# An mLSTM and gated feed-forward kernel: the opening's order of work is rewritten

## The chip, the cores and the metric

The kernel runs on one core of one Trainium2 chip. The metric is the device time of one execution in microseconds, the median of several runs; smaller is better. The engines are named as in the profile: PE (TensorE, matmuls and transposes), PEld (its weight loads), DVE (VectorE), ACT (ScalarE), POOL (GpSimd) and SP (SyncE, which issues the DMAs).

## The reference

Two steps, both in fp32. The first is an mLSTM over 4 batches, 8 heads, 768 time steps and a head size of 40:

```python
for t in range(S):
    kt, vt, qt = (k[:, :, t], v[:, :, t], q[:, :, t])
    m_new = np.maximum(f_gate[:, :, t] + m, i_gate[:, :, t])
    f_stab = np.exp(f_gate[:, :, t] + m - m_new)
    i_stab = np.exp(i_gate[:, :, t] - m_new)
    m = m_new
    C = f_stab[:, :, None, None] * C + i_stab[:, :, None, None] * np.einsum('bhd,bhe->bhde', vt, kt)
    n = f_stab[:, :, None] * n + i_stab[:, :, None] * kt
    h_tilde = np.einsum('bhde,bhe->bhd', C, qt)
    nq = np.einsum('bhd,bhd->bh', n, qt)[:, :, None]
    denom = np.maximum(np.abs(nq), 1.0)
    o = 1.0 / (1.0 + np.exp(-o_gate[:, :, t]))
    y[:, :, t] = o * h_tilde / denom
```

Its output, 3072 tokens of 320 numbers (batch by time), goes through a gated feed-forward:

```python
gate = 1.0 / (1.0 + np.exp(-(x @ w_gate)))
val = x @ w_val
return (gate * val @ w_out).astype(np.float32)
```

with an inner width of 1536.

## The kernel before, in words

The 768 time steps are cut into 6 chunks of 128. A chunk of one batch is a *unit*: unit n is chunk n // 4 of batch n % 4, so units 0 to 3 are the first chunk of batches 0 to 3. Inside a chunk the recurrence is done as attention: scores of q and k (128 x 128 per head), multiplied with a decay matrix `d`, then with v; a state of 40 x 41 per head is carried from chunk to chunk. The feed-forward works on the output of a chunk, 128 or 256 or 512 tokens wide, in 12 blocks of 128 of the inner width. In the first chunk the first four blocks are done for batches 0 and 1 alone, as soon as these are there.

All matmuls of the feed-forward are exact enough for fp32 by a split in two: each operand x is written as `xh` (rounded) and `xl` (the rest), and three products are summed. The same holds for the weights, which arrive as raw 64-bit words and are unpacked in the kernel.

The order of all work is written out by hand: the table `ORDER` (L47 on) is a string of names, and the kernel emits the operation of each name in that order. Each engine then runs its own operations in that order, one behind the other, and waits by semaphores for what others produce. The table `eng` in `PARAM` says for some names which engine does it ('v' DVE, 'p' POOL, 'a' ACT). The number behind a name is the unit, the weight piece or the feed-forward block. The names that matter here:

- `ee3.0`, `ee3.1` (L657, ACT): exponents of the decay matrix of batch 3, four heads each, in place in the tile `d_3`, which a DMA fills (`d<-mscr`). `em3` (L671, POOL) then sets the upper triangle to zero; `kw3` (L881, POOL) multiplies unit 3's k with a column of it.
- `tr` (L762, PE) and `cp` (L770 on ACT, L772 on DVE): the transposes of q and k of a unit, and the copies of them out of PSUM.
- `s` (L690, PE): scores; `t` (L872, DVE): scores times decay; `av` (L938, PE): times v; `cs` (L1014, PE) and `cm` (L1043, ACT): the state.
- `nd`, `ns`, `ro` (L951 to L962, DVE): the output gate and the denominator; `ro` writes the tile `x`. `xd` (L987): a copy of 64 columns inside `x`; `xt` (L993, PE): transposes of `x` into PSUM; `xh` (L1000, ACT) and `xl` (L1004, DVE): the two parts, input of the feed-forward.
- `u0`, `u1` (L1070, PE): three products of two matmuls each with the gate weights (`u0`) or the value weights (`u1`); `r0`, `r1` (L1074, L1075): the last 64 rows of them. `th` (L1080, ACT), `gx` (L1087, DVE), `gh` (L1092, ACT), `gl` (L1097, DVE): the gate, the product and its two parts; `dn` (L1107 to L1109, PE): the second matmul, three products, of which the third needs `gl`.
- weights: `wa` (L517, ACT), `wb` (L521, DVE), `wc` (L526, DVE), `wo` (L531, DVE) unpack a piece into the staging tile `dc`; `wh` (L543, ACT) writes the rounded part and `wl` (L548, POOL) the rest. The piece is named behind: g gate weights, v value weights, r the last rows, o the output weights (whose two parts are shown as `oh` and `ol`); `wlo1` is the rest of output piece 1.
- `gm5`, `gd` (L427, L428, L438, DVE): the running maximum of the gates over the chunks; `tb` (L448 on PE, L453 on DVE): its transposes.
- `wk` (L404, PE): bf16 matmuls on zeros, spread over the opening, which write a PSUM tile that nobody reads. `wm` (L394, PE): eight fp32 matmuls on zeros, likewise.

Buffers are handed out in turn by the helpers `sbt` and `pst`: a name with k buffers gets them one after the other in the order of the table, and whoever takes a buffer waits for the readers of its last content. The staging tiles `dc` have 3 buffers; the PSUM tiles of `tr`, `s` and `tb` (tag `pa`) have 2; `x` has one. The tile `sg` of block 0, which `th0` writes, has the place in SBUF where the padded k of unit 3 lies before, which `kw3` reads.

Of the kernel before, what the change touches and what calls it, by code (L numbers as in the profile page):

```python
# [37 lines left out]
    'NW': 12,  # L38
    'eng': {
# [3 lines left out]
    },  # L43
}
# [4 lines left out]
    wav0 lk0 gc tap tac sp0.1 ee0.0 lk1 gm1 sp1.0 wco0 lq1 wcr0 ee0.1 kw0 lo0 tr0.1 wor0 whr0 wbv0 wlr0 gm2 lv0 i5  # L49
    tr0.0 sp1.1 cp0.0 cp0.1 s0.0 tr1.0 woo0 wdo4 gm3 lo1 ee1.0 ee1.1 cp1.0 wdo1 ld2 l10 tr1.1 kw1 wcv0 wov0 t0.0 lv1  # L50
    lq3 wdg0 cp1.1 wao4 tr2.0 l11 cp2.0 s1.0 who0 gm4 cs0 wlo0 wbo4 wco4 t0.1 whv0 av0 t1.0 og1 wlv0 og0 cm0.1 t1.1
    lk2 wao1 ld3 wbo1 woo4 ee2.1 who4 wco1 wlo4 woo1 wk4 av1 ee2.0 wdg1 em2 nd0 ns0 gs1 wk5 cm0.0 ro0 wk6 wdo3 wag0
    nd1 ns1 tr3.0 cp3.0 xd0 wbg0 lk3 lv2 l12 tr2.1 xt0 cp2.1 ro1 wcg0 kw2 ee3.1 wk7 xh0 wk8 who1 wk9 gm5 xd1 i8 wk10
    lo2 xt1 wdr1 wog0 xh1 xl0 wk11 xl1 wag1 ld4 wdv1 wbg1 wm gd s2.0 t2.0 t2.1 whg0 u1.0 r1.0 wlo1 tbp tbc wlg0
    tr3.1 lq4 wao3 wbo3 cp3.1 ee3.0 u0.0 r0.0 war1 og2 em3 lv3 kw3 lo3 th0 wco3 wcg1 woo3 wdo5 cs1 wbr1 cm1.1 who3
    wlo3 lk4 wog1 gx0 cm1.0 whg1 gh0 lq5 av2 ns2 ee4.0 u0.1 ee4.1 gl0 r0.1 th1 dn0.0 nd2 l13 wcr1 ro2 s3.0 wor1 t3.0
    t3.1 wlg1 u1.1 r1.1 wav1 wbv1 cs2 wcv1 wdv3 wao5 wbo5 u0.2 wov1 xd2 cm2.1 tr4.0 wco5 cm2.0 em4 cp4.0 gx1 whv1
# [1104 lines left out]
```

## Time and profile before

| what | value |
|---|---|
| median of 3 runs | 518.9 us (518.62 to 519.23) |
| span of the profiled execution | 517.4 us (the 1.5 us to the median lie around the span) |
| PE busy | 506.7 us (98%) |
| PEld busy | 468.3 us (91%) |
| DVE busy | 332.8 us (64%) |
| ACT busy | 242.1 us (47%) |
| POOL busy | 246.3 us (48%) |
| chain that ended last | PE 89%, DMA 5%, ACT 2%, DVE 2% |

The profile lists, for one execution, what each engine did and when; the span is the time from its first to its last instruction. Starts are counted from the beginning of the span. An operation that stands as x4 is four instructions in a row, and the duration is that of all of them together. In brackets behind a row stands the idle time of the engine before it and what ended it. Starts of neighbouring rows can lie closer than the first one's duration, because an engine takes up the next instruction while the last one is still finishing.

### The profile page before, as it was taken

The numbers are of one execution on the slowest core, as the hardware profiler recorded it, in microseconds if no ns is written. First come the engines' busy times: TensorE is split into PE (matmuls) and PEld (weight loads), VectorE is DVE, ScalarE is ACT, GpSimd is POOL, SyncE is SP. The second block draws the span as 40 slices with busy tenths as digits, with TensorE's granted clock in tenths as the row PEclk, the third lists the DMA queues.
The fourth block names the chain that finished last, engine by engine and source line by source line (L and its number), as shares of the span: only waits on it lengthen the run. The fifth ranks groups of instructions, "written<-read, shape, count | busy, mean of one in ns | idle before, by whom it ended". The sixth has DMA issues, their size and how long they took to land.

```text
span 517.4 us, 11006 instructions
## 1 busy us (share of the span) xinstructions
PE 506.7 (98%) x4020; PEld 468.3 (91%) x4021; DVE 332.8 (64%) x699; ACT 242.1 (47%) x560; POOL 246.3 (48%) x272
## 2 busy tenths in 40 slices
PE   6989999999999999999999999999999999999997
PEld 4789988889999999998888888898888888999996
DVE  7978877785776677678766456856445474642332
ACT  4887766554444354644444443353344324232322
POOL 3656546557146686459536544187315504510000
PEclk9999999999999999999999999999999999999999
DMA  8999875339687797799879787599465835220000
GB/s 196 259 231 225 223 201 141 102 95 178 135 185 156 166 203 163 162 205 158 171 138 178 181 153 141 135 181 185 96 146 102 173 81 111 65 58 1 1 27 27
DMA packets 222478, 74.17 MB, mean 143 GB/s; under 512 B 167380, under 2 KB 214168, under 8 KB 222424
## 3 DMA queue, kind: packets, MB, share of 16 engines
q1 hardware_dynamic: 221336, 73.20, 64.8%
q8 instruction: 32, 0.52, 0.4%
q10 hardware_dynamic: 1088, 0.26, 0.2%
q14 instruction: 22, 0.18, 0.1%
HBM read 61.54 MB, written 11.90 MB: 142 GB/s over the span
## 4 chain that ended last, share of the span: by engine, by line
PE 89%; DMA 5%; ACT 2%; DVE 2%; issue 1%; SPq 1%; POOL 0%; POOLq 0%; DVEq 0%; ACTq 0%
PE pg L1070 38%; PE po L1107 8%; PE po L1109 8%; PE po L1108 7%; PE pg L1074 6%; PE pg L1075 6%; PE av L931 3%; PE s L753 2%; PE av L938 2%; DMA d<-mscr 2%; PE in L914 2%; PE cs L1014 2%; PE s L808 1%; DMA st_v<-in_moe_w_val_dram 1%; DMA scx<-tx 1%
## 5 line engine op out<-in xcount | busy, mean ns | idle before, releaser
L1092 ACT ACTIVATE gh<-pg 128x256 fp32r<-128x256 f32 (+1 forms) x103 | 48.2, 468 | 142.9 <-DVE pg L1087 120.7
L1087 DVE SCALAR_TENSOR_TENSOR pg<-sg,pg 128x256 f32<-128x256 f32 (+1 forms) x103 | 54.8, 532 | 92.1 <-PE pg L1075 75.4
L1070 PE MATMUL pg<-xh,wh 128*128 128x256 f32 (+1 forms) x412 | 104.8, 336 | 0.2 <-ACT xh L1000 0.2
L1070 PE MATMUL pg<-xh,wl 128*128 128x256 f32 (+1 forms) x412 | 100.9, 326 | 0.0
L1070 PE MATMUL pg<-xl,wh 128*128 128x256 f32 (+1 forms) x412 | 100.8, 326 | 0.0
L1107 PE MATMUL po<-oh,gh 128*128 128x320 f32 x288 | 92.6, 322 | 0.0
L1109 PE MATMUL po<-oh,gl 128*128 128x320 f32 x288 | 89.1, 309 | 0.1
L1108 PE MATMUL po<-ol,gh 128*128 128x320 f32 x288 | 88.9, 309 | 0.0
L1080 ACT ACTIVATE sg<-pg 128x256 f32<-128x256 f32 (+1 forms) x103 | 48.1, 467 | 73.3 <-PE pg L1075 71.9
L1097 DVE TENSOR_TENSOR gl<-pg,gh 128x256 fp32r<-128x256 f32 (+1 forms) x103 | 54.3, 527 | 36.6 <-ACT gh L1092 34.9
L1070 PEld LDWEIGHTS pg<-xl,wh 128*128 128x128 f32 x412 | 69.1, 189 | 7.3 <-POOL xl L1004 0.3
L1070 PEld LDWEIGHTS pg<-xh,wl 128*128 128x128 f32 x412 | 69.0, 189 | 7.1
L1070 PEld LDWEIGHTS pg<-xh,wh 128*128 128x128 f32 x412 | 67.7, 189 | 3.7 <-DVE gl L1097 0.6
L1074 PE MATMUL pg<-xh,w 128*128 128x256 f32 (+1 forms) x206 | 68.5, 333 | 0.0
L1075 PE MATMUL pg<-xl,w 128*128 128x256 f32 (+1 forms) x206 | 67.0, 326 | 0.0
L1107 PEld LDWEIGHTS po<-oh,gh 128*128 128x128 f32 x288 | 54.4, 189 | 2.5
L1108 PEld LDWEIGHTS po<-ol,gh 128*128 128x128 f32 x288 | 54.2, 188 | 2.6
L1109 PEld LDWEIGHTS po<-oh,gl 128*128 128x128 f32 x288 | 54.1, 188 | 0.7 <-DVE gl L1097 0.6
L671 POOL TENSOR_SCALAR_AFFINE_SELECT d<-d 128x1024 f32<-128x1024 f32 x22 | 26.2, 1192 | 52.6 <-ACT d L667 51.9
L887 POOL TENSOR_TENSOR dr<-d 128x1024 f32<-128x1024 f32 x16 | 30.3, 1894 | 35.7 <-DVE d L872 35.3
L872 DVE TENSOR_TENSOR d<-s,d 128x384 f32<-128x384 f32 (+2 forms) x68 | 34.9, 527 | 14.5 <-PE s L753 8.9
L1075 PEld LDWEIGHTS pg<-xl,w 128*128 128x128 f32 x206 | 39.0, 189 | 2.7
(159 smaller groups left out, 886.2 us busy)
## 6 DMA issues: line engine op xcount, KB each, us to landing
d<-mscr SPq DMA_DIRECT2D x22, 512.0 KB
ks<-scq SPq DMA_DIRECT2D x48, 168.0 KB
qs<-scq SPq DMA_DIRECT2D x48, 168.0 KB
scq<-tq SPq DMA_DIRECT2D x64, 80.0 KB
su_o<-in_moe_w_out_dram SPq DMA_DIRECT2D x12, 320.0 KB
o<-in_o_gate_dram SPq DMA_DIRECT2D x24, 160.0 KB
v<-in_v_dram SPq DMA_DIRECT2D x24, 160.0 KB
out_dram<-ob SPq DMA_DIRECT2D x24, 160.0 KB
```

Source lines behind the costliest of these rows:

```text
L872: nc.vector.tensor_tensor(y, ps_[n, g][:, :nh, :], y, ALU.mult)
L887: E("da", n).tensor_tensor(dr[n][0], dm[n], top(dm[n]), ALU.subtract)
L1070: nc.tensor.matmul(p, w[y][:, a, fs], x[c][:, a, n0:n1], start=(i + a == 0), stop=False)
L1074: nc.tensor.matmul(pg[n, y], w2[y][:, fs], xh[c][:, 2, n0:n1], start=False, stop=False)
L1075: nc.tensor.matmul(pg[n, y], w2[y][:, fs], xl[c][:, 2, n0:n1], start=False, stop=True)
L1080: nc.scalar.activation(s, pg[n, 0], AF.Tanh, scale=0.5)
L1087: nc.vector.scalar_tensor_tensor(sgs[n], gate, 1.0, pg[n, 1], ALU.add, ALU.mult)
L1092: nc.scalar.activation(ghs[n][:, :nt], sgs[n], AF.Copy)
L1097: E("gl", n).tensor_tensor(gls[n][:, :nt], sgs[n], ghs[n][:, :nt].bitcast(F32), ALU.subtract)
L1107: nc.tensor.matmul(p, ghs[n][:, ts], oh[:, j, :], start=(j == 0), stop=False)
L1108: nc.tensor.matmul(p, ghs[n][:, ts], ol[:, j, :], start=False, stop=False)
L1109: nc.tensor.matmul(p, gls[n][:, ts], oh[:, j, :], start=False, stop=(j == NF - 1))
```

## The change

Four lines of the order table are rewritten, one name gets another engine, and one name is left out:

```diff
--- before.py
+++ after.py
@@ -38,7 +38,7 @@
     'NW': 12,
     'eng': {
         'gl': 'v', 'ca': 'v', 'ro': 'v', 'cm': 'a', 'cp0': 'a', 'cp2': 'a', 'qb2': 'v', 'dl0': 'v', 'cp11': 'a',
-        'qb00': 'v', 'qb10': 'v', 'qb20': 'v', 'qb01': 'v', 'qb21': 'p', 'xd0': 'v', 'ea0': 'a', 'ea1': 'a', 'ea2': 'a',
+        'qb00': 'v', 'qb10': 'v', 'qb20': 'v', 'qb01': 'v', 'qb21': 'p', 'xd0': 'v', 'xd1': 'v', 'ea0': 'a', 'ea1': 'a', 'ea2': 'a',
         'ea3': 'a', 'pz': 'v', 'gc': 'v', 'gd': 'v', 'ea4': 'a', 'ea5': 'a', 'ea6': 'a', 'ea7': 'a',
     },
 }
@@ -49,9 +49,9 @@
     wav0 lk0 gc tap tac sp0.1 ee0.0 lk1 gm1 sp1.0 wco0 lq1 wcr0 ee0.1 kw0 lo0 tr0.1 wor0 whr0 wbv0 wlr0 gm2 lv0 i5
     tr0.0 sp1.1 cp0.0 cp0.1 s0.0 tr1.0 woo0 wdo4 gm3 lo1 ee1.0 ee1.1 cp1.0 wdo1 ld2 l10 tr1.1 kw1 wcv0 wov0 t0.0 lv1
     lq3 wdg0 cp1.1 wao4 tr2.0 l11 cp2.0 s1.0 who0 gm4 cs0 wlo0 wbo4 wco4 t0.1 whv0 av0 t1.0 og1 wlv0 og0 cm0.1 t1.1
-    lk2 wao1 ld3 wbo1 woo4 ee2.1 who4 wco1 wlo4 woo1 wk4 av1 ee2.0 wdg1 em2 nd0 ns0 gs1 wk5 cm0.0 ro0 wk6 wdo3 wag0
-    nd1 ns1 tr3.0 cp3.0 xd0 wbg0 lk3 lv2 l12 tr2.1 xt0 cp2.1 ro1 wcg0 kw2 ee3.1 wk7 xh0 wk8 who1 wk9 gm5 xd1 i8 wk10
-    lo2 xt1 wdr1 wog0 xh1 xl0 wk11 xl1 wag1 ld4 wdv1 wbg1 wm gd s2.0 t2.0 t2.1 whg0 u1.0 r1.0 wlo1 tbp tbc wlg0
+    lk2 wao1 ld3 wbo1 woo4 ee2.1 who4 wco1 wlo4 woo1 wk4 av1 ee2.0 wdg1 em2 nd0 ns0 gs1 wk5 cm0.0 ro0 xd0
+    wk6 wdo3 xt0 wag0 nd1 ns1 ro1 lk3 lv2 l12 xd1 xt1 xh0 wbg0 xl0 tr3.0 xh1 cp3.0 xl1 tr2.1 cp2.1 wcg0 kw2 wk7 wk8
+    wk9 gm5 i8 wk10 lo2 wdr1 wog0 wk11 who1 ld4 wdv1 whg0 wlg0 u1.0 r1.0 wag1 wbg1 ee3.1 gd s2.0 t2.0 t2.1 wlo1 tbp tbc
     tr3.1 lq4 wao3 wbo3 cp3.1 ee3.0 u0.0 r0.0 war1 og2 em3 lv3 kw3 lo3 th0 wco3 wcg1 woo3 wdo5 cs1 wbr1 cm1.1 who3
     wlo3 lk4 wog1 gx0 cm1.0 whg1 gh0 lq5 av2 ns2 ee4.0 u0.1 ee4.1 gl0 r0.1 th1 dn0.0 nd2 l13 wcr1 ro2 s3.0 wor1 t3.0
     t3.1 wlg1 u1.1 r1.1 wav1 wbv1 cs2 wcv1 wdv3 wao5 wbo5 u0.2 wov1 xd2 cm2.1 tr4.0 wco5 cm2.0 em4 cp4.0 gx1 whv1
```

`xd1`, the 64-column copy of unit 1, goes from POOL to DVE. The names `xd0 xt0 nd1 ns1 ro1 xd1 xt1 xh0 xl0 xh1 xl1` come ahead of `tr3.0`, `cp3.0`, `tr2.1`, `cp2.1` and `ee3.1`. `u1.0 r1.0` come ahead of `s2.0`. `whg0 wlg0` come ahead of `u1.0`, `wag1`, `ee3.1` and `wlo1`. `wm` is dropped.

On ACT, from `wag0` (`dc_g<-st_g`) to `war1` (`dc_r`), before:

```order
L517 ACTIVATE dc_g_387<-st_g_288 128x512
L770 ACTIVATE qkt_399<-pt_0_394 128x512
L657 ACTIVATE d_342<-d_342,at 128x128 x4
L1000 ACTIVATE xh_427<-xt_412 128x3x128
L543 ACTIVATE oh<-dc_o_340 128x320
L1000 ACTIVATE xh_427<-xt_441 128x3x128
L517 ACTIVATE dc_g_453<-st_g_369 128x512
L543 ACTIVATE wh_100<-dc_g_387 128x2x256
L517 ACTIVATE dc_o_508<-su_o_385 128x320
L657 ACTIVATE d_342<-d_342,at 128x128 x4
L517 ACTIVATE dc_r_525<-su_r_445 128x256
```

and now:

```order
L517 ACTIVATE dc_g_392<-st_g_288 128x512
L1000 ACTIVATE xh_410<-xt_388 128x3x128
L1000 ACTIVATE xh_410<-xt_406 128x3x128
L770 ACTIVATE qkt_421<-pt_0_415 128x512
L543 ACTIVATE oh<-dc_o_340 128x320
L543 ACTIVATE wh_100<-dc_g_392 128x2x256
L517 ACTIVATE dc_g_464<-st_g_369 128x512
L657 ACTIVATE d_342<-d_342,at 128x128 x4
L517 ACTIVATE dc_o_499<-su_o_386 128x320
L657 ACTIVATE d_342<-d_342,at 128x128 x4
L517 ACTIVATE dc_r_516<-su_r_443 128x256
```

`qkt` is `cp3.0`, the two L657 rows are `ee3.1` and `ee3.0`, the L1000 rows `xh0` and `xh1`, `oh` is `who1`, `wh_100` is `whg0`, and `dc_o` behind the exponents is `wao3`. Both `xh` now stand ahead of `ee3.1`, which stands behind `whg0` and `wag1`; `wao3` still follows it. In these rows and the next the number behind a tile tells which of several it is; it differs between the two kernels.

On POOL, from `kw2` (k of unit 2) to `wlg1`, before:

```order
L881 TENSOR_TENSOR k_420<-pad_97,d_272 128x320
L987 COPY x_417<-x_417 128x64
L548 TENSOR_TENSOR ol<-dc_o_340,oh 128x320
L548 TENSOR_TENSOR wl_101<-dc_g_387,wh_100 128x2x256
L671 AFFINE_SELECT d_342<-d_342 128x1024
L881 TENSOR_TENSOR k_531<-pad_99,d_342 128x320
L548 TENSOR_TENSOR ol<-dc_o_508,oh 128x320
L609 MEMSET v_529 128x8
L548 TENSOR_TENSOR wl_101<-dc_g_453,wh_100 128x2x256
```

and now:

```order
L881 TENSOR_TENSOR k_431<-pad_97,d_272 128x320
L548 TENSOR_TENSOR wl_101<-dc_g_392,wh_100 128x2x256
L548 TENSOR_TENSOR ol<-dc_o_340,oh 128x320
L671 AFFINE_SELECT d_342<-d_342 128x1024
L881 TENSOR_TENSOR k_522<-pad_99,d_342 128x320
L548 TENSOR_TENSOR ol<-dc_o_499,oh 128x320
L609 MEMSET v_520 128x8
L548 TENSOR_TENSOR wl_101<-dc_g_464,wh_100 128x2x256
```

The copy `xd1` is gone from POOL, and `wlg0` (`wl_101`) stands ahead of `wlo1` (`ol`), where it stood behind it.

On DVE, the twelve rows that end with `t2.0` and `t2.1` (L872), before:

```order
L772 COPY qkt_299<-pt_1_407 128x512
L962 TENSOR_TENSOR x_417<-o_257,den_389 128x320
L526 TENSOR_SCALAR dc_g_387<-dc_g_387 128x512
L427 SCALAR_TENSOR_TENSOR mg<-gin,mend 32x128
L428 TENSOR_TENSOR mend<-gin,mg 32x1
L531 SCALAR_TENSOR_TENSOR dc_g_387<-st_g_288,dc_g_387 128x512
L1004 TENSOR_TENSOR xl_428<-xt_412,xh_427 128x3x128
L1004 TENSOR_TENSOR xl_428<-xt_441,xh_427 128x3x128
L521 TENSOR_SCALAR dc_g_453<-dc_g_453 128x512
L438 TENSOR_TENSOR gin<-mend,mg 32x640
L872 TENSOR_TENSOR d_272<-s_0_470,d_272 128x4x128
L872 TENSOR_TENSOR d_272<-s_1_471,d_272 128x4x128
```

and now:

```order
L521 TENSOR_SCALAR dc_g_392<-dc_g_392 128x512
L1004 TENSOR_TENSOR xl_411<-xt_388,xh_410 128x3x128
L1004 TENSOR_TENSOR xl_411<-xt_406,xh_410 128x3x128
L772 COPY qkt_299<-pt_1_424 128x512
L526 TENSOR_SCALAR dc_g_392<-dc_g_392 128x512
L427 SCALAR_TENSOR_TENSOR mg<-gin,mend 32x128
L428 TENSOR_TENSOR mend<-gin,mg 32x1
L531 SCALAR_TENSOR_TENSOR dc_g_392<-st_g_288,dc_g_392 128x512
L521 TENSOR_SCALAR dc_g_464<-dc_g_464 128x512
L438 TENSOR_TENSOR gin<-mend,mg 32x640
L872 TENSOR_TENSOR d_272<-s_0_472,d_272 128x4x128
L872 TENSOR_TENSOR d_272<-s_1_473,d_272 128x4x128
```

The two `xl` (L1004) have moved ahead of `cp2.1` (`qkt`); what follows `cp2.1` (`wcg0`, the two rows of `gm5`, `wog0`, then `wbg1`, `gd`) is in the order in which it was.

## Rows read from the trace of the kernel before

**Rows 1.** Busy time of each engine in three stretches; columns as the header line says.
```profile
core 0: us, PE busy (x) PEld busy (x) DVE busy (x) ACT busy (x) POOL busy (x), PEclk, DMA share, GB/s
8.00:12.00 4.00, 2.56 (x20) 2.11 (x19) 3.90 (x13) 3.07 (x11) 0.29 (x1) 1.00 1.11 201
20.00:30.00 10.00, 8.09 (x59) 6.31 (x60) 7.61 (x24) 7.13 (x21) 4.32 (x6) 1.00 0.94 246
30.00:40.00 10.00, 10.00 (x98) 9.41 (x95) 8.92 (x23) 8.31 (x27) 6.84 (x8) 1.00 0.94 236
```

**Rows 2.** Chain of waits, 18 to 40 us: start, duration, what.
```profile
20.04 6.59 DMA d<-mscr
...
29.07 0.57 DVE xl L1004
```

**Rows 3.** Timeline of PE, 22 to 40 us: start, duration, line, operation, out<-in, count.
```profile
25.11 0.76 PE L993 MATMUL xt<-ident,x 128*128 128x128 f32 x3
...
25.93 1.95 PE L394 MATMUL pwarm<-warm 128*128 128x128 f32 x16
...
30.77 0.51 PE L1070 MATMUL pg<-xh,wh 128*128 128x256 f32 x2
...
31.92 0.49 PE L448 MATMUL tbt<-ident,gin 32*128 32x32 f32 x5
...
32.75 0.48 PE L1070 MATMUL pg<-xh,wh 128*128 128x256 f32 x2
...
37.40 0.33 PE L1109 MATMUL po<-oh,gl 128*128 128x320 f32 x1
```

**Rows 4.** Timeline of ACT, 20 to 40 us; in brackets the idle time before.
```profile
28.94 0.66 ACT L517 ACTIVATE dc_g<-st_g 128x512 f32<-128x512 f32 x1
29.51 0.61 ACT L543 ACTIVATE wh<-dc_g 128x512 fp32r<-128x512 f32 x1
30.03 0.48 ACT L517 ACTIVATE dc_o<-su_o 128x320 f32<-128x320 f32 x1
30.41 1.26 ACT L657 ACTIVATE d<-d,at 128x128 f32<-128x128 f32 x4
...
34.02 0.38 ACT L1080 ACTIVATE sg<-pg 128x256 f32<-128x256 f32 x1 [0.71 <-POOL k L881]
```

**Rows 5.** Timeline of DVE, 21 to 40 us.
```profile
21.85 0.49 DVE L962 TENSOR_TENSOR x<-o,den 128x320 f32<-128x320 f32 x1
...
23.97 0.69 DVE L772 COPY qkt<-pt 128x512 f32<-128x512 f32 x1 [0.20 <-PE pt L762]
...
24.97 0.42 DVE L526 TENSOR_SCALAR dc_g<-dc_g 128x512 int32<-128x512 int32 x1
...
25.89 0.67 DVE L531 SCALAR_TENSOR_TENSOR dc_g<-st_g,dc_g 128x512 int32<-128x512 int32 x1
...
29.63 0.43 DVE L521 TENSOR_SCALAR dc_g<-dc_g 128x512 f32<-128x512 f32 x1
...
30.74 1.29 DVE L872 TENSOR_TENSOR d<-s,d 128x512 f32<-128x512 f32 x2
...
36.84 0.42 DVE L1097 TENSOR_TENSOR gl<-pg,gh 128x256 fp32r<-128x256 f32 x1
```

**Rows 6.** Timeline of POOL, 20 to 40 us.
```profile
28.75 0.87 POOL L548 TENSOR_TENSOR ol<-dc_o,oh 128x320 fp32r<-128x320 f32 x1 [3.26 <-ACT oh L543]
30.20 1.75 POOL L548 TENSOR_TENSOR wl<-dc_g,wh 128x512 fp32r<-128x512 f32 x1 [0.58 <-ACT wh L543]
...
33.08 0.74 POOL L881 TENSOR_TENSOR k<-pad,d 128x320 f32<-128x320 f32 x1
```

**Rows 7.** Timeline of all engines, 99.0 to 99.6 us: DVE beside POOL.
```profile
99.21 1.29 POOL L548 TENSOR_TENSOR wl<-dc_g,wh 128x512 fp32r<-128x512 f32 x1
...
99.42 1.44 DVE L962 TENSOR_TENSOR x<-o,den 128x320 f32<-128x320 f32 x1
```

**Rows 8.** Timeline of PE, 0 to 25 us: keep-warm matmuls.
```profile
2.81 1.87 PE L404 MATMUL pkeep<-warm 128*128 128x512 bf16 x4 [2.81 <-ACT warm L317]
...
24.23 1.03 PE L404 MATMUL pkeep<-warm 128*128 128x512 bf16 x4
```

## The prediction

> **What bounds the kernel now.** I read the busy times of a few stretches first. In the stretch from 20 to 30 us PE is busy for 8.09 of 10 us, and from 30 to 40 for all 10.00 [rows 1]; on the page PE is busy for 98% of the span. So nearly all of the end time is PE work, and an opening that hands PE its first feed-forward block later or earlier is carried to the end, unless a later wait of PE absorbs it. The few waits left later on are short and depend on other things, so I carry the whole shift.
>
> The chain of work through 18 to 40 us says what PE waits for there. The load of batch 3's `d` ends it: 6.59 us of DMA from 20.04 [rows 2]. Behind it ACT does `ee3.1`, then both `xh`, and `xl1` on DVE ends at 29.64 [rows 2]. On PE this shows as follows [rows 3]: `xt1` at 25.11, the eight matmuls on zeros at 25.93 (1.95 us, as 16 records), then scores, and `u1.0` only at 30.77. From there on PE is dense: `tb` at 31.92, `u0.0` at 32.75 and the third matmul of `dn0.0` at 37.40.
>
> **The change part by part.**
>
> *The matmuls on zeros.* They take 1.95 us from 25.93 [rows 3], and PE could do nothing else there, since `xl0` was not ready. Their price is 0 now. If the feed-forward comes forward they would be in its way, so leaving them out belongs to the next step and is not counted twice. The cover is gone too: PE then idles in later gaps, which is the third rival.
>
> *`xh` and `xl` ahead of `ee3.1`.* `u1.0` no longer waits for the DMA. On DVE, `ro0` starts at 21.85 and `wcg0` at 24.97 [rows 5], with seven small pieces between. In the new order the 0.69 us of `cp2.1` [rows 5] leave that stretch and `xd1` comes in, so `xd1` ends at about 24.3. `xt1` takes 0.76 [rows 3], to 25.05; its `xh` and `xl` end by 25.8. PE has `tr3.0` and `tr2.1` (each a group like `xt1`, some 0.6), then five keep-warm matmuls, 1.03 per four [rows 8], before `u1.0`: 25.05 + 1.2 + 1.1 = 27.4. That is 3.4 us ahead of 30.77, and is the upper bound of the gain.
>
> *What takes that gain back on DVE.* `u1.0` and `r1.0` are some 1.15 us of work (30.77 to 31.92 [rows 3]), then `s2.0` some 1.1, so PE has reached `tb` by 29.7. `tb` and `tr3.1` need the two PSUM buffers that the scores fill, and these come free with `t2.0` and `t2.1` on DVE. Now `cp2.1` stands behind both `xl`: it begins when `tr2.1` is through, at about 26.3, and ends at 27.0. Then `wcg0`, `gm5` and `wog0` follow, 1.59 us by their old rows (24.97 to 25.89 + 0.67 [rows 5]): 28.6. `whg0` on ACT takes 0.61 to 29.26, and `wag1`, which now stands behind it, 0.66 more, to about 29.86 [rows 4]. `wbg1`, `gd` and `t2` follow on DVE as before: `t2` starts 1.11 behind `wbg1` (29.63 to 30.74 [rows 5]), at 31.0, and both parts take 1.29, to 32.3. Then `tr3.1` and, 0.41 behind it (the distance from 31.92 to 32.75 holds two such pieces [rows 3]), `u0.0` at 32.75. It stood at 32.75 before. The early `u1.0` has become an idle stretch of about 2 us on PE, from 29.7 on; worth 0.
>
> *The new wait on POOL.* Before, `wlo1` (0.87 at 28.75) ran ahead of `wlg0` (at 30.20) [rows 6]. Now `wlg0` is first, and it cannot start before `whg0` is done, at 29.3. `wlo1` is queued behind it though its own input is ready. And `wao3` on ACT writes the staging buffer that `wlo1` reads (`dc` has three buffers, and `dc_o3` falls on that of `dc_o1`). So `wao3` waits: 29.3 + `wlg0` + 0.87. A `wl` of this shape takes 1.29 us when it runs alone [rows 7], and took 1.75 at 30.20 [rows 6]; that gives 31.45 or 31.9, against 30.03 before [rows 4], a shift of 1.4 to 1.9. I take the 1.29: the 1.75 fell behind `gd`, which had begun 0.2 us earlier, and here `wlg0` starts before it.
>
> *What is queued behind `wao3`.* `ee3.0` on ACT (1.26 at 30.41 [rows 4]), `em3` on POOL, `kw3` (0.74 at 33.08 [rows 6]), and then `th0`: its tile `sg0` lies where unit 3's k lay, which `kw3` reads last. The row of `th0` shows 0.71 us of waiting for POOL already before the change, at 34.02 [rows 4]. From `wao3` to `th0` that is 34.02 - 30.03 = 3.99 us, without slack: each piece starts when the one before ends. So `th0` moves by the same 1.4 to 1.9. From `th0` to `gl0` it was 2.82 us (36.84 - 34.02 [rows 5]), of which up to 0.3 were waits of the state copies on PE that vanish when `th0` is late. `dn0.0`'s third matmul came 0.56 after `gl0`'s start. It moves from 37.40 by 1.1 at least and 1.9 at most.
>
> Nothing else that the blocks need is late: SP's and PE's DMA and weight order stays, `war1` waited 0.82 us for its DMA at 32.49 and now has slack, and `xd1` on DVE instead of POOL costs DVE 0.2 us that is in the chain above.
>
> **The sum.** 0 for the matmuls, 0 for the early `u1.0`, +1.4 at `dn0.0`. The profiled execution has a span of 517.4 us, and the median of the runs is 518.9; the 1.5 us around the span I leave as they are. So 518.9 + 1.4 = **520.3 us**, from 520.0 to 520.8 in its own case. A difference of 0.2%, 1.04 us, is about what can be told from no change.
>
> **The port.** What can add to this is in another part of the trace: at 99.42 `ro` on DVE, usually 0.49 [rows 5], took 1.44, and ended only after the `wl` on POOL that had begun at 99.21 [rows 7]. So an operation of DVE that meets a `wl` already running is held. In the change `wlg0` (29.3 to 30.6) begins before `wbg1` (29.9). Held, `wbg1` would end near 30.9, `wlo1` would go next, to 31.8, and `gd` behind it; `t2` at 32.4 instead of 31.0, `u0.0` at 34.4, and PE is 1.65 late at 34.4 already: 520.6 to 520.9. The Trainium skill, page "SBUF — State Buffer", section "Who interferes with whom", says the same as a rule: of VectorE and GpSimd on the shared port pair, the one that issues first gets it for the whole instruction, and the other fully blocks. By that rule the time would be the 520.6 to 520.9 of this case; the row at 99.42 agrees with it, the row at 30.20 (`wl` at 1.75 behind `gd`) too.
>
> **The rivals.**
> 1. *Nothing is lost on POOL (519.0).* If `cp2.1` runs about 1.2 us earlier than I put it, `whg0` starts by 27.4 and `wlo1` ends by 30.2; then `wao3` is where it was, `th0` too, and the time stays within some 0.3 us of 518.9. For it: the stretch from 24.3 to 26.3 holds waits that I only bounded. Against it: `wcg0` to `wog0` wait in DVE's queue for `cp2.1`, and `cp2.1` for PE's transposes behind `xt1`. The point from which it decides is `whg0` at 27.4. In between, at 28.0, the loss is some 0.7, which also counts as no change. Chance 0.28.
> 2. *The early start is kept (faster).* If `t2` and `th0` both come early, PE keeps what `u1.0` gains: 3.4 us at most, 515.5; half of that, 517.2, where only `u0.0` comes forward. For it: `u1.0` is early for certain, and PE had 1.9 us idle from 20 to 30 [rows 1]. Against it: `t2` needs `gd` in DVE's order, and `th0` hangs on `kw3`, which needs `ee3.0` behind `wao3`. Chance 0.08.
> 3. *The clock falls (522).* The first four keep-warm matmuls took 1.87 us, those at 24.23 took 1.03 [rows 8]: at the start PE ran at about half pace, later at full. Without the matmuls on zeros PE idles for 2 us before `tb`. A slow spell twice as long as the first of these rows, 3.7 us, loses half of it, 1.85: 520.3 + 1.85 = 522.1. Against it: from 8 to 12 us PE was busy for only 2.56 of 4 us, and the granted clock stood at 1.00 [rows 1]. The Trainium skill, page "TensorE: Matmul & The Clock Gate", section "What's actually happening", has idleness bring the slow level, 1.2 instead of 2.4 GHz; by it the time would be the 522 of this rival, and the row from 8 to 12 us does not bear it out for gaps of this size. Chance 0.04.
> 4. The held port, as above: chance 0.14 apart from the forecast's own case.
>
> That the change does not do what it says I leave out: the order shows `u1.0` ahead of the scores and `ee3.1` behind `whg0`.
>
> **How the numbers follow.** The forecast's case (+1.1 to +1.9) has 0.46, the held port 0.14, no loss 0.28, kept gain 0.08, the clock 0.04. Slower by over 0.2%: 0.46 + 0.14 + 0.04 = 0.64, where I leave the lower edge of the first case out of account. Same: 0.28. Faster: 0.08. The range leaves out the kept gain and the clock, and reaches from just below no loss, 518.8, to the held port with the longer `wl`, 521.2.
>
> **What would show it right or wrong.** Right: `u1.0` at about 27.4; PE idle for 1.5 to 2.5 us between `s2.0` and `tr3.1`, released by `t2` on DVE; `u0.0` at 32.5 to 34.5; ACT's `wao3` waiting for POOL `ol` at about 31.5; `th0` waiting for `kw3` until 35.4 or later; PE's third `dn0.0` matmul waiting for `gl0` at 38.5 to 39.2; and from there every row shifted by the same amount. Wrong: `whg0` at 27.4 or earlier, `wao3` that does not wait, or `th0` at 34 us. If `wbg1` or `gd` is longer than its rows before, the port case is the right one. If the granted clock is below 1.00 in the stretch from 28 to 40 us, rival 3 is.

## The result, and the profile after

The changed kernel takes **524.3 us** (median of 6 runs, 521.3 to 528.8), the kernel before in the same comparison 518.8 (6 runs, 518.2 to 519.2). The ratio is 1.0116, 95% interval 1.0077 to 1.0155: slower, by 5.5 us, where 1.4 was forecast and 521.2 was the upper end of the range. The runs of before lie within 1 us, those of the change within 7.5, and the time goes with the mean granted clock of the run: 521.3 at 0.997, 521.8 and 523.3 at 0.992, 525.2 at 0.990, 527.5 at 0.983, 528.8 at 0.976. The last one is the profiled execution, with a span of 527.1 us; the loss in it is therefore larger than in the median.

Busy times of the changed kernel in stretches of 2 us, columns as in [rows 1] (length, busy time of each engine, PEclk, share of DMA, GB/s):

```profile
core 0: us, PE busy (x) PEld busy (x) DVE busy (x) ACT busy (x) POOL busy (x), PEclk, DMA share, GB/s
...
22.00:24.00 2.00, 0.84 (x4) 0.34 (x3) 1.89 (x6) 1.51 (x5) 1.52 (x3) 1.00 0.90 224
24.00:26.00 2.00, 1.00 (x4) 0.66 (x5) 1.64 (x4) 0.25 (x2) 0.40 (x1) 0.54 0.96 336
...
28.00:30.00 2.00, 2.00 (x7) 0.81 (x5) 1.88 (x5) 0.00 (x0) 0.00 (x0) 0.50 0.69 123
...
32.00:34.00 2.00, 0.62 (x12) 0.43 (x8) 2.00 (x3) 1.32 (x5) 1.31 (x2) 1.00 0.81 252
34.00:36.00 2.00, 1.35 (x8) 1.29 (x9) 1.77 (x4) 1.71 (x6) 0.92 (x1) 0.60 1.17 284
...
40.00:42.00 2.00, 2.00 (x12) 2.00 (x11) 0.00 (x0) 2.00 (x8) 1.59 (x3) 0.50 0.92 190
...
48.00:50.00 2.00, 2.00 (x12) 2.00 (x12) 1.97 (x6) 0.00 (x0) 0.00 (x0) 0.50 0.00 0
50.00:52.00 2.00, 2.00 (x14) 2.00 (x13) 1.23 (x4) 1.23 (x6) 0.00 (x0) 0.64 0.00 0
```

PEclk is 1.00 up to 24 us, 0.50 from then on, 1.00 again from 31 us on, and falls a second time, at about 34.4 us, to come back only at about 51.5. In [rows 1] it is 1.00 in every stretch. 0.50 is the 1.2 GHz level, 1.00 the 2.4 GHz level. Ahead of both falls stands a stretch in which PE is little busy: 0.84 of 2 us from 22 to 24, and 0.62 of 2 from 32 to 34. From 36 to 50 us PE is busy all the time, at half pace. Such a stretch does not always bring a fall: the kernel before has one too, from 28 to 30 us, and keeps 1.00.

```profile
28.00:30.00 2.00, 0.77 (x6) 0.61 (x8) 1.48 (x4) 2.00 (x5) 0.87 (x1) 1.00 0.68 125
```

The changed kernel on PE's timeline (start, duration, line, what; in brackets the idle time before):

```profile
23.19 0.33 PE L993 MATMUL xt<-ident,x 128*128 128x128 f32 x1 [0.50 <-DVE x L987]
24.89 0.87 PE L993 MATMUL xt<-ident,x 128*128 128x128 f32 x3 [1.37 <-DVE x L962]
25.87 2.17 PE L762 MATMUL pt<-ident,pad 128*128 128x128 f32 x8
27.84 2.34 PE L404 MATMUL pkeep<-warm 128*128 128x512 bf16 x5
29.62 0.99 PE L1070 MATMUL pg<-xh,wh 128*128 128x256 f32 x2
...
34.65 0.73 PE L448 MATMUL tbt<-ident,gin 32*128 32x32 f32 x5 [2.02 <-DVE d L872]
...
36.08 0.78 PE L1070 MATMUL pg<-xh,wh 128*128 128x256 f32 x2
...
44.76 0.47 PE L1109 MATMUL po<-oh,gl 128*128 128x320 f32 x1
```

Against [rows 3]: `xt1` starts at 24.89 after two idle times (0.50 behind `xd0`, 1.37 behind `ro1`); the two transposes behind it take 2.17 us for eight pieces, and the five keep-warm matmuls 2.34, where four took 1.03 in [rows 8]. `u1.0` starts at 29.62, only 1.15 us earlier than before instead of 3.4. Then `tb` waits 2.02 us for `t2` on DVE, `u0.0` starts at 36.08 (32.75 before) and `dn0.0`'s third matmul at 44.76 (37.40 before): 3.3 us are lost at `u0.0`, 7.4 at `dn0.0`. The last 4 are made by no wait; that work is dense in both kernels and ran at half clock here.

DVE, POOL and ACT in the same stretch, one fence each:

```profile
22.16 0.97 DVE L987 COPY x<-x 128x64 f32<-128x64 f32 x1
...
28.09 0.69 DVE L772 COPY qkt<-pt 128x512 f32<-128x512 f32 x1 [1.21 <-PE pt L762]
...
31.53 1.06 DVE L521 TENSOR_SCALAR dc_g<-dc_g 128x512 f32<-128x512 f32 x1 [1.25 <-ACT dc_g L517]
32.51 1.48 DVE L438 TENSOR_TENSOR gin<-mend,mg 32x640 f32<-32x640 f32 x1
33.92 1.27 DVE L872 TENSOR_TENSOR d<-s,d 128x512 f32<-128x512 f32 x2
```

```profile
21.94 1.14 POOL L671 TENSOR_SCALAR_AFFINE_SELECT d<-d 128x1024 f32<-128x1024 f32 x1 [0.30 <-ACT d L657]
...
31.02 1.29 POOL L548 TENSOR_TENSOR wl<-dc_g,wh 128x512 fp32r<-128x512 f32 x1 [6.62 <-ACT wh L543]
32.27 1.04 POOL L548 TENSOR_TENSOR ol<-dc_o,oh 128x320 fp32r<-128x320 f32 x1
```

```profile
33.35 0.49 ACT L517 ACTIVATE dc_o<-su_o 128x320 f32<-128x320 f32 x1 [0.68 <-POOL ol L548]
...
38.22 0.39 ACT L1080 ACTIVATE sg<-pg 128x256 f32<-128x256 f32 x1 [2.52 <-issue]
```

Three operations of DVE are long: `xd0` 0.97 us (0.22 for unit 0's copy before), behind `em2`, which runs on POOL from 21.94 to 23.08; `wbg1` 1.06 (0.43 in [rows 5]), behind `wlg0` from 31.02 on; `gd` 1.48 (0.81 before), behind `wlo1` from 32.27. `wao3` (33.35) waits for `wlo1`, as forecast, but for 0.68 us only, and `th0` comes at 38.22 (34.02 in [rows 4]).

### The profile page after: what moved, and what is told of

Same layout as the page of the kernel before. It is cut to its first block, busy times and chain, and to the rows that moved or that the text cites. A ratio compares the mean times of both kernels' runs of the same rounds, so it can differ in the third digit from the quotient of the medians.

```text
span 527.1 us, 10976 instructions
## 1 busy us (share of the span) xinstructions
PE 514.8 (98%) x4005; PEld 475.4 (90%) x4005; DVE 334.4 (63%) x700; ACT 242.8 (46%) x560; POOL 246.0 (47%) x271
## 4 chain that ended last, share of the span: by engine, by line
PE 90%; DVE 4%; ACT 2%; DMA 2%; issue 1%; SPq 1%; DVEq 0%; ACTq 0%
PE pg L1070 38%; PE po L1107 8%; PE po L1109 8%; PE po L1108 8%; PE pg L1074 6%; PE pg L1075 6%; PE av L931 3%; PE s L753 2%; PE av L938 2%; PE cs L1014 2%; PE in L914 2%; PE s L808 1%; DMA st_v<-in_moe_w_val_dram 1%; DVE x L962 1%; ACT d L635 1%
## 5 line engine op out<-in xcount | busy, mean ns | idle before, releaser
L1070 PE MATMUL pg<-xh,wh 128*128 128x256 f32 (+1 forms) x412 | 106.3, 340 | 0.1
L1070 PE MATMUL pg<-xh,wl 128*128 128x256 f32 (+1 forms) x412 | 102.1, 329 | 0.0
L1070 PEld LDWEIGHTS pg<-xl,wh 128*128 128x128 f32 x412 | 70.3, 193 | 7.1
L1070 PEld LDWEIGHTS pg<-xh,wl 128*128 128x128 f32 x412 | 70.2, 192 | 7.0
L1070 PEld LDWEIGHTS pg<-xh,wh 128*128 128x128 f32 x412 | 69.0, 192 | 3.9 <-DVE gl L1097 0.9
L872 DVE TENSOR_TENSOR d<-s,d 128x384 f32<-128x384 f32 (+2 forms) x68 | 35.0, 527 | 17.8 <-PE s L753 8.3
```

Source lines behind the costliest of these rows:

```text
L872: nc.vector.tensor_tensor(y, ps_[n, g][:, :nh, :], y, ALU.mult)
L1070: nc.tensor.matmul(p, w[y][:, a, fs], x[c][:, a, n0:n1], start=(i + a == 0), stop=False)
```

## The experiments

Two theories stand against each other. *Clock:* the loss is made by the two idle stretches on PE, after which the granted clock falls. *Order:* it is made by the waits of the new order, at full clock too. All kernels are compared with runs of before on the same chip, which differ by more than a microsecond from chip to chip (medians 519.06 to 520.33). Where I give a time "at full clock", it is the median of the runs with a mean clock of 0.999 or more.

**1. Fill both idle stretches.** Fifteen more bf16 matmuls on zeros (`NW` 27), which nobody reads:

```diff
- xd1 xt1
+ xd1 wk12 wk13 wk14 wk15 wk16 wk17 xt1
...
- wlo1 tbp
+ wlo1 wk18 wk19 wk20 wk21 wk22 wk23 wk24 wk25 wk26 tbp
```

> The changed kernel with 15 more bf16 keep-warm matmuls on PE, 6 ahead of xt1 and 9 ahead of tb, where it idled 1.4 and 2.0 us. Nothing else is moved. Clock theory: the loss and the spread come from the granted clock falling after these two gaps; with them filled the clock stays at 1.00 and the time falls to 520.0 to 520.8, the price of the order alone (DVE's chain, the wait of wao3 for wlo1, operations held behind POOL), with a spread of the runs under 1 us. Rival, the order's waits alone: they are as long as in the changed kernel, the time stays at 522 or more.

Measured: 522.6 (6 runs, 522.1 to 523.5), ratio 1.0063 [1.0042, 1.0084]; clock 1.00 in five of the six runs. The spread shrinks from 7.5 us to 1.4, and to 0.7 among the five (under 1 was expected); the time is not as expected: at full clock 522.45 against 518.94 for before, 3.5 us instead of 1.0 to 1.8. So both theories hold a part: most of the spread goes with the clock, and 3.5 us remain at full clock. The added matmuls make little of these: `tb` still waits 1.44 us for DVE behind the nine. PE, DVE and ACT in its profile:

```profile
33.25 0.49 PE L444 MATMUL tbt<-ident,gin 32*128 32x32 f32 x5 [1.44 <-DVE d L868]
...
34.26 0.48 PE L1066 MATMUL pg<-xh,wh 128*128 128x256 f32 x2
...
38.99 0.41 PE L1105 MATMUL po<-oh,gl 128*128 128x320 f32 x1
```

```profile
30.13 1.05 DVE L517 TENSOR_SCALAR dc_g<-dc_g 128x512 f32<-128x512 f32 x1 [1.26 <-ACT dc_g L513]
31.11 1.48 DVE L434 TENSOR_TENSOR gin<-mend,mg 32x640 f32<-32x640 f32 x1
32.52 1.27 DVE L868 TENSOR_TENSOR d<-s,d 128x512 f32<-128x512 f32 x2
```

```profile
35.62 0.39 ACT L1076 ACTIVATE sg<-pg 128x256 f32<-128x256 f32 x1 [1.33 <-POOL k L877]
```

`wbg1` and `gd` are held as in the change, `t2` comes at 32.52, `u0.0` at 34.26, `th0` at 35.62, `dn0.0`'s third matmul at 38.99.

**2. One stretch at a time.** The first fill alone (`NW` 18), the second alone (`NW` 21, nine matmuls), and the eight fp32 matmuls back:

```diff
- xd1 xt1
+ xd1 wk12 wk13 wk14 wk15 wk16 wk17 xt1
```

> The changed kernel with 6 keep-warm matmuls ahead of xt1 only; the 2 us gap ahead of tb stays. If the first gap (behind xt0) is what lets the clock fall: no spell at 24 to 31 us, and the runs lie near those of the kernel with both gaps filled, 522 to 523.5, mean clock 0.997 or more. If the gap ahead of tb does it too: a spell from 34 us on in most runs, time 523 to 528.

```diff
- wlo1 tbp
+ wlo1 wk12 wk13 wk14 wk15 wk16 wk17 wk18 wk19 wk20 tbp
```

> The changed kernel with 9 keep-warm matmuls ahead of tb only; the gap behind xt0 stays. If the first gap decides: a spell from about 24 to 31 us at half clock in most runs, mean clock 0.993, time 522.5 to 525; no spell after 34 us. If only the gap ahead of tb counted: clock 1.00 and 522.5.

```diff
- wlg0 u1.0
+ wlg0 wm u1.0
```

> The changed kernel with the eight fp32 matmuls on zeros put back, ahead of u1.0. If their removal is what lets the clock fall: clock 1.00, time near 520.5. If the gaps ahead of them (22.7 to 24.9 us, behind xt0 and ahead of xt1) are the cause: the first fall at 24 us stays, the gap ahead of tb shrinks to under 0.5 us, and the second spell at half clock (34 to 51 us) shortens or vanishes; time 520.5 to 523.

With the first stretch filled: 525.4 (12 runs, 523.2 to 530.0), 1.0108 [1.0073, 1.0143], clock 0.984 to 0.997. With the second filled: 523.6 (12 runs, 523.0 to 525.8), 1.0069 [1.0045, 1.0094], clock 0.989 to 0.997. With `wm` back: 523.6 (6 runs, 522.8 to 526.0), 1.0091 [1.0063, 1.0118], clock 0.992 or 0.993 in all runs. No run of these three kept the full clock; with both stretches filled five of six did. The stretch ahead of `tb` is the dearer one: filling it takes away most of the spread. `wm` back shrinks it to 0.85 us but costs `u1.0` its early start and does nothing for the first. One trace does not fit the clock theory as it stands. With the second stretch alone filled, the clock falls at about 21.9 us, ahead of the first idle stretch, while PE is busy:

```profile
20.00:22.00 2.00, 2.00 (x18) 1.79 (x18) 1.86 (x7) 2.00 (x8) 0.88 (x1) 0.97 0.87 274
```

**3. The eight matmuls alone, taken from the kernel before.**

```diff
- wbg1 wm gd
+ wbg1 gd
```

> The kernel before without the eight fp32 matmuls on zeros, nothing moved. Prediction's step (they only cover idle time, worth 0): 518.8 plus or minus 0.4, clock 1.00. Clock theory in its simple form (their removal uncovers a gap of 3 us from 25.9 to 29.05): the clock falls near 28 us, time 520 to 526 with a wide spread.

Measured: 520.7 (12 runs, 519.1 to 522.6) against 519.06, ratio 1.0029 [1.0011, 1.0046]. The ratio is little above the 0.2% by which before differs from itself in experiment 7; the clock says more: 11 of the 12 runs have a mean clock below 0.999, where 4 of 17 of before have. Its one trace shows a slow spell too, though ahead of the place where `wm` stood. It begins at about 21.2 us, in a stretch in which PE is busy all the time:

```profile
20.00:22.00 2.00, 2.00 (x17) 1.96 (x17) 1.86 (x7) 2.00 (x9) 0.94 (x2) 0.80 0.93 278
22.00:24.00 2.00, 1.96 (x9) 1.16 (x7) 1.48 (x7) 1.34 (x5) 1.43 (x3) 0.50 0.99 219
```

How the removal leads to more slow spells was not seen in a trace and stays open.

**4. Where the second spell ends.** Nine keep-warm matmuls in a stretch where PE is busy anyway; both gaps left open (`NW` 21):

```diff
- r0.0 war1
+ r0.0 wk12 wk13 wk14 wk15 wk16 wk17 wk18 wk19 wk20 war1
```

> The changed kernel with 9 keep-warm matmuls behind u0.0 and r0.0, in a stretch where PE is busy anyway; both gaps stay open. They cost 2 us at full clock. [...] Rival (what PE does there has no bearing on the spell): spells to 51 us as before, time 526 to 531.

Measured: 527.6 (4 runs, 526.0 to 528.5), clock 0.986 to 0.994. That is slower than the 524 to 526 expected if these matmuls end the spell early, and within the rival's range. Windows and PE rows:

```profile
34.00:36.00 2.00, 1.50 (x10) 1.44 (x10) 1.77 (x4) 1.55 (x5) 1.06 (x1) 0.50 1.18 220
...
38.00:40.00 2.00, 1.77 (x5) 0.67 (x5) 1.12 (x3) 0.38 (x1) 0.00 (x0) 0.50 0.45 91
40.00:42.00 2.00, 2.00 (x15) 1.42 (x13) 0.00 (x0) 0.12 (x1) 0.00 (x0) 0.86 0.21 81
42.00:44.00 2.00, 2.00 (x20) 2.00 (x20) 0.37 (x1) 2.00 (x8) 0.96 (x3) 1.00 0.52 90
```

```profile
38.23 3.04 PE L399 MATMUL pkeep<-warm 128*128 128x512 bf16 x8 [0.24 <-issue]
```

The spell that began at 33.7 us ends at about 40.6, while these matmuls run (38.23 to 41.27), and not at 51. In the changed kernel PE did fp32 work all that time and the clock stayed low. But that is one trace of each, and in the trace with the first stretch alone filled the second spell ended by itself, at 37.8 us after 3.4, in the same fp32 work. So its length varies from run to run, and that the matmuls ended it is not shown.

**5. Which wait makes the order's price.** All four have the idle stretches filled as in the first experiment (the last with three matmuls ahead of `tb`); what is moved:

`wlo1` back ahead of `wlg0`:

```diff
- whg0 wlg0 u1.0
+ whg0 wlo1 wlg0 u1.0
```

> As the first of these kernels (filled gaps), and wlo1 back ahead of wlg0 on POOL. Prediction's wait of wao3: th0 comes 1.3 us earlier than in the first kernel and the time falls by 0.7 to 1.5 us against it. Rival (DVE's chain and the operations held behind POOL bind, not wao3): time within 0.3 us of the first kernel, u0.0 unchanged.

`wbg1` behind `t2`, so that `gd` and `t2` wait neither for `whg0` and `wag1` nor for POOL:

```diff
- wag1 wbg1 ee3.1 gd s2.0 t2.0 t2.1
+ wag1 ee3.1 gd s2.0 t2.0 t2.1 wbg1
```

> The kernel with both gaps filled, and on DVE wbg1 moved behind t2, so that gd and t2 no longer stand behind whg0, wag1 and wbg1 and gd is not held behind wlo1. Theory (DVE's chain to t2 binds): t2 starts at 29.7 instead of 32.5 us, u0.0 near 32.4 instead of 34.3, and the time falls by 1.0 to 2.0 against the kernel with both gaps filled (522.5). Rival (th0 behind kw3 and ee3.0 binds): u0.0 is earlier but dn0.0 is not, and the time falls by less than 0.5.

The exponents ahead of `whg0`, and `wlo1` ahead of `wlg0`:

```diff
- whg0 wlg0 u1.0 r1.0 wag1 wbg1 ee3.1 gd
+ ee3.1 ee3.0 whg0 wlo1 wlg0 u1.0 r1.0 wag1 wbg1 gd
...
- cp3.1 ee3.0 u0.0
+ cp3.1 u0.0
```

> The kernel with both gaps filled, with ee3.1, ee3.0 ahead of whg0 on ACT and wlo1 ahead of wlg0 on POOL; DVE's order left as in the change (gd and t2 behind wag1 and wbg1). The chain over kw3 to th0 is mended, the one to t2 is not. Theory (both chains bind about equally): th0 no longer waits for kw3 but for u0.0, which starts at 34 us or later, and the time stays within 0.5 of the kernel with both gaps filled (3 to 3.5 us over before). Rival (the chain to th0 alone was the price): 519.5 to 520.5, 0.5 to 1 over before.

All of these at once, `gd` right behind `wog0`, and `xd0` and `xt0` behind `ns1`:

```diff
- ro0 xd0 wk6 wdo3 xt0 wag0 nd1 ns1 ro1
+ ro0 wk6 wdo3 wag0 nd1 ns1 xd0 xt0 ro1
...
- wog0 wk11
+ wog0 gd wk11
...
- whg0 wlg0 u1.0 r1.0 wag1 wbg1 ee3.1 gd s2.0 t2.0 t2.1 wlo1
+ ee3.1 ee3.0 whg0 wlo1 wlg0 u1.0 r1.0 wag1 s2.0 t2.0 t2.1 wbg1
```

> The changed kernel with its waits taken out by order: ee3.1 and ee3.0 ahead of whg0 on ACT, wlo1 ahead of wlg0 on POOL, gd right behind wog0 and wbg1 behind t2 on DVE, xd0 behind ns1; and keep-warm matmuls, 6 ahead of xt1 and 3 ahead of tb. Theory (the order's price at full clock is two chains, DVE's to t2 and ACT's and POOL's over ee3.0 to th0, which both have to go): u0.0 at 31 to 32.5, th0 at 33 to 34, no wait of PE at dn0.0, clock 1.00, time 518 to 519.3, 3 us under the kernel with both gaps filled. Rival (the price lies in something else, the early xh and xl or the later transposes): 521 or more.

| kernel | median (runs) | ratio to before | at full clock, it and before |
|---|---|---|---|
| filled | 522.58 (6) | 1.0063 [1.0042, 1.0084] | 522.45, 518.94 |
| + `wlo1` first | 522.46 (6) | 1.0063 [1.0040, 1.0086] | 522.02, 518.94 |
| + `wbg1` behind `t2` | 523.02 (12) | 1.0053 [1.0026, 1.0081] | 522.41, 519.45 |
| + exponents and `wlo1` first | 524.53 (7) | 1.0091 [1.0058, 1.0124] | 522.89, 519.13 |
| all | 521.14 (11) | 1.0002 [0.9981, 1.0023] | 520.71, 519.71 |

Moving `wlo1` alone gives 0.4 us, inside its noise. With `wbg1` behind `t2`, `u0.0` is earlier, and PE then waits for `gh0`, because `th0` waits for `kw3`. (The traces do not start alike: the two keep-warm matmuls ahead of `xt0` begin at 22.11 here and at 21.06 in the first filled kernel. Counted from them `u0.0` is 1.7 us earlier and `th0` where it was.) ACT and PE of that kernel:

```profile
36.69 0.38 ACT L1076 ACTIVATE sg<-pg 128x256 f32<-128x256 f32 x1 [1.49 <-POOL k L877]
```

```profile
33.63 0.48 PE L1066 MATMUL pg<-xh,wh 128*128 128x256 f32 x2
...
39.28 0.41 PE L1103 MATMUL po<-oh,gh 128*128 128x320 f32 x1 [0.98 <-ACT gh L1088]
```

With the exponents first, `th0` no longer waits for `kw3`, and `tb` and `u0.0` are late as ever, `u0.0` even 1.2 us later than in the first filled kernel, counted from the same two matmuls (21.52 here). So this kernel does not leave the chain to `t2` as it was:

```profile
34.91 0.49 PE L444 MATMUL tbt<-ident,gin 32*128 32x32 f32 x5 [2.10 <-DVE d L868]
...
35.91 0.48 PE L1066 MATMUL pg<-xh,wh 128*128 128x256 f32 x2
...
40.57 0.34 PE L1105 MATMUL po<-oh,gl 128*128 128x320 f32 x1
```

Only with both chains mended does PE get on:

```profile
30.88 0.49 PE L443 MATMUL tbt<-ident,gin 32*128 32x32 f32 x5
...
31.89 0.48 PE L1065 MATMUL pg<-xh,wh 128*128 128x256 f32 x2
...
37.52 0.41 PE L1104 MATMUL po<-oh,gl 128*128 128x320 f32 x1
```

That fits two chains that bind about equally: each alone gives 0.6 us or nothing, both give 2.5 us of the 3.5 (from 3.51 over before to 1.00 at full clock). The last kernel also moves `xd0` and adds six matmuls fewer, so the share of each edit is not shown. It was expected to end at 518 to 519.3, and missed that by 1.4, of which 0.8 is the chip (before 519.71 there, 518.94 on the first). In its trace the opening is level with before, 0.1 us late at `dn0.0`, but the span is 2.5 us longer. The longest wait of its PE behind 40 us, at 235 us, is:

```profile
PE s L748 <- DVE t L914: 1.0, 1, 1.0
```

Neither trace of before has it; whether the order or the run made it is not known.

**6. The order mended, no matmuls on zeros added.**

The edit is that of the last kernel, without the `wk` names.

> The same order as the one before it, without any added keep-warm matmul (and without wm, as in the changed kernel). Theory (the long spells at half clock come from the idle stretch ahead of tb, which the order makes): the stretch shrinks to under 1 us, the spell from 34 us on is gone; the one from 24 to 31 us, behind the gap ahead of xt1, stays in most runs; mean clock 0.993 to 0.997, time 519 to 521. Rival (any leaving out of zero matmuls brings the long spells): 523 to 528 as in the changed kernel.

Measured: 521.7 (12 runs, 520.5 to 523.6), 1.0026 [1.0005, 1.0047], clock 0.989 to 0.997. The stretch ahead of `tb` is 0.85 us in its trace, and the clock is at 0.50 there only from about 25.5 to 29 us. The upper half of the changed kernel's runs, 525 to 529, does not occur. The long spells go with the idle stretch ahead of `tb` that the order made: a mean clock of 0.984 or less has 2 of 6 runs of the changed kernel and 4 of 12 with the first stretch alone filled, and none of the 30 runs of the three kernels in which this stretch is filled or down to 0.85 us (second filled, `wm` back, and this one).

Counted over all experiments, 0.999 or more was kept by 27 of 42 runs of the five kernels that have matmuls added in both stretches, by none of the 52 runs of the changed kernel and its five versions without them in one or both, and by 56 of 98 runs of before. Filling is no warrant: in the trace of the kernel with `wlo1` first the clock falls at 23.3 us all the same, and its six added matmuls ahead of `xt1` take 2.77 us instead of 1.46.

**7. Can either kernel be beaten.** First the kernel before in another order:

```diff
- ro1 wcg0 kw2 ee3.1 wk7 xh0 wk8 who1 wk9 gm5 xd1
+ ro1 xd1 xh0 wcg0 kw2 wk7 wk8 wk9 gm5
...
- wog0 xh1 xl0 wk11 xl1 wag1 ld4 wdv1 wbg1 wm gd s2.0 t2.0 t2.1 whg0 u1.0 r1.0 wlo1 tbp tbc wlg0 tr3.1 lq4 wao3
+ wog0 xh1 xl0 who1 wlo1 wk11 xl1 ee3.1 ld4 wdv1 gd s2.0 t2.0 t2.1 whg0 wlg0 wag1 wk12 wk13 u1.0 r1.0 wk14 wk15
+ tbp tbc tr3.1 lq4 ee3.0 wbg1 wao3
```

> The kernel before with another order: both xh and who1 ahead of ee3.1 on ACT, xd1 on DVE, s2.0 right behind xt1, gd and t2 ahead of u1.0 and of wbg1 on DVE, ee3.0 ahead of wao3, wlo1 ahead of wlg0; wm left out and four keep-warm matmuls more. Theory (what holds PE back after 27 us is DVE's chain to t2 and the one over ee3.0 and kw3 to th0, and cp2.1 stays early here): u0.0 at 30 to 31 us, th0 at 32.5 to 33.5, third dn0.0 matmul at 36 to 36.8, clock 1.00; time 517.5 to 518.3 against 519. Rival (the clock falls or an operation is held behind POOL): 519 to 521.

Measured: 520.2 (12 runs) against 519.65, 0.9994 [0.9966, 1.0022]: no difference. In its trace the load of a pad ended PE's idle time ahead of `tr2.1` 1.77 us long (0.54 in before, there ended by ACT), the clock fell near 29 us, and `u0.0` came at 34.0, not 30 to 31. Then before with its own gaps filled, and before itself:

```diff
- l12 tr2.1
+ l12 wk17 wk18 tr2.1
...
- wm gd
+ wm wk12 wk13 wk14 wk15 wk16 gd
```

> The kernel before with 7 keep-warm matmuls more: 5 behind the eight fp32 ones, where PE idled 1.2 us, and 2 ahead of tr2.1, where it idled 0.5. Clock theory (a quarter of the runs of before have a mean clock of 0.993 and take 521 to 525): with these gaps filled such runs become rare, the median falls by 0.3 to 0.8 and the upper tail goes. Rival (the slow tail of before comes from elsewhere, DMAs that are late): same median and tail.

> The kernel before itself, for a second trace. If the small losses at 70, 261 and 378 us (0.4 to 0.8 each) that the kernels with filled gaps show against the first trace of before are the run's luck, this trace shows some of them too; if the change makes them, none. Time: the same as before, ratio 1.000.

Filled: 519.35 against 519.35 (12 and 24 runs), 0.9997 [0.9979, 1.0015]; all runs at 0.997 or more, but no faster. Before itself, built once more: 518.4 (12 runs), 0.9979 [0.9961, 0.9996]; so a kernel against itself can come out 0.2% off, and ratios of that size say nothing here. Its second trace shows the two things it was run for. The clock falls in it as well, behind 1.96 us in which PE waited for the load of a pad, and little is lost: ACT waits for the load of `d` until 26.28 us as it did in the first trace, and `u0.0` comes at 33.13 us (32.75).

```profile
22.00:24.00 2.00, 0.51 (x5) 0.27 (x3) 1.46 (x7) 1.55 (x5) 1.15 (x2) 1.00 0.72 199
24.00:26.00 2.00, 1.53 (x8) 1.50 (x9) 0.41 (x1) 0.00 (x0) 0.73 (x1) 0.54 0.96 331
26.00:28.00 2.00, 2.00 (x9) 1.02 (x8) 1.97 (x6) 1.72 (x6) 0.37 (x1) 0.61 1.09 301
28.00:30.00 2.00, 2.00 (x19) 1.91 (x16) 1.96 (x5) 2.00 (x5) 1.03 (x2) 1.00 0.53 94
```

And PE waits for `gl` at `dn` after 40 us, which the first trace does not show. Waits by releaser (us in total, times, longest), this trace and the filled kernel of the first experiment:

```profile
PE po L1109 <- DVE gl L1097: 0.3, 2, 0.2
```

```profile
PE po L1105 <- DVE gl L1093: 0.6, 3, 0.2
```

No version is faster than the kernel before.

## Why the prediction was wrong

Two steps failed. By the first experiment, a comparison of its own, the order costs 3.5 us at full clock, where 1.4 was forecast; that alone ends above 521.2, the upper end of the range. The rest of the 5.5 us, about 2, is left for the clock in the median run.

- **The clock** is the one step, left out of the sum: "Against it: from 8 to 12 us PE was busy for only 2.56 of 4 us, and the granted clock stood at 1.00 ... Chance 0.04", at a price of 1.85 us for one slow spell. Both falls of the changed kernel came behind idle stretches, and filling these kept the clock in 27 of 42 runs, leaving one or both open in none of 52; a single stretch without a fall was no proof that such stretches are safe. What sets off a single fall is not shown: two traces fall while PE is busy (21.2 and 21.9 us), and before keeps 1.00 behind 0.77 us of work in 2. The second spell lasted 17 us in the profiled run, through work that was dense before and after. At half pace this cost 4 us between `u0.0` and `dn0.0` alone, more than twice the 1.85. The rule of the Trainium skill cited there (page "TensorE: Matmul & The Clock Gate", section "What's actually happening": idleness brings the 1.2 GHz level) had the direction right; the two falls of the changed kernel agree with it, those at 21.2 and 21.9 us show no idle stretch of PE right ahead of them.
- **A gap not seen.** The prediction named the idle time ahead of `tb` (2 us, measured 2.02) but not the one ahead of `xt1`. `xt0` and `xt1` now stand in front of the transposes and the keep-warm matmuls, so that PE idles while DVE does `xd0`, `nd1`, `ns1`, `ro1` and `xd1`. The first spell begins there, and it lengthens the very pieces that `cp2.1` waits for: `cp2.1` at 28.09 where 26.3 was forecast (26.68 with the gaps filled, in a trace that starts 0.66 us early, see below).
- **The same spell in before is hidden.** In the second trace of before the clock fell at about the same time, while `ee3.1` and all behind it waited for the load of `d` anyway. The prediction read that wait as lost time only; it was also the cover for a slow clock. This is argued from one trace of each, and it does not cover every spell: the 14 runs of before with a mean clock of 0.993 or less took 518.6 to 524.4, with a median of 522.4.
- **"0 for the matmuls"** is doubtful: taking them from before alone costs 0.29%, interval 0.11 to 0.46%, little more than before against itself, but the clock stays up in 1 run of 12 instead of 13 of 17.
- **The DVE chain** is the other step, right in kind and wrong in size: `u1.0` came at 27.37 at full clock (27.4 forecast), but `u0.0`, forecast at 32.75 from operations of their usual length, came at 34.26. The trace even starts early: the keep-warm matmuls ahead of `xt0` begin at 21.06, those at the same place in before at 21.72. Counted from them `u0.0` is 2.2 us later than in before. What was left for a rival, the held port, happened: `t2` at 32.4 and `u0.0` at 34.4 were worked out there, 32.52 and 34.26 were measured, with `wbg1` at 1.05 and `gd` at 1.48 us. `xd0` was held besides, which that rival did not have; that its times were met so closely is in part luck, from the early start. The rule of the Trainium skill (page "SBUF — State Buffer", section "Who interferes with whom") that the later one fully blocks agrees with these rows, and should have been in the forecast's own sum.
- **`wao3` behind `wlo1`** exists (0.68 us) but is not the price. `th0` came at 35.62 at full clock, inside the forecast's 35.4 to 35.9 (again with the early start); by the runs it is late because `ee3.1` and `ee3.0` stand behind `whg0`, which stands behind `cp2.1` and `wog0`. The prediction had this chain and hung it on the wrong piece.
- **The sum at full clock**: 3.5 us against 1.4, and "I carry the whole shift" did not hold either. In the trace of the filled kernel `dn0.0`'s third matmul is 1.6 us later than in before (2.25, counted from the same two matmuls), and the span is 3.7 longer. The difference grows behind the opening, in part at matmuls of `dn` that wait for `gl`, which before's second trace has too. That trace is 0.4 us late at `dn0.0` and 0.9 at the end, so some of this is the run's and not the order's; how much is not shown. The mended kernel, which is level with before at `dn0.0`, ends 1.0 behind at full clock as well.

## What to carry to other kernels

Before moving a unit of work forward, look at what PE does while it waits for it: a PE that idles for a microsecond or two (here 1.9 and 2.0) can run at half its clock for many microseconds of dense work behind it (here 7 and 17), and the price is paid there, not in the gap. A wait that looks like pure loss may hide a slow clock, and matmuls on zeros in it may be earning something; test them by taking them out alone. Where two chains end at nearly the same time, mending one may show nothing, so mend both before giving a theory up.

## What was not expected of the hardware

The granted clock stayed at 0.50 for 17 us in which PE was busy without a break with fp32 matmuls (34.4 to 51.5). In a second kernel it rose after 6.8 us, while eight bf16 matmuls on zeros, 3.04 us long, ran, and in a third after 3.4 us of fp32 work at the same place. Its falls are not the same from run to run: the changed kernel's mean clock went from 0.976 to 0.997 in six runs of one program, and the kernel before fell to 0.992 or 0.993 in some runs on each of the four chips of the experiments.
